# Sign of converted 64-bit weights: carried by ScalarE's slope for negative numbers instead of a VectorE step

## The chip, the cores and the metric

The kernel runs on one core of a Trainium2 chip. The metric is the device time of one execution in microseconds (us). Each time is told with its source: the median of several runs, or one profiled execution with its trace.

## The reference

All inputs are drawn on the host; what is computed is

```python
scores = scale * np.matmul(q, k.transpose(0, 1, 3, 2))      # q, k, v: (4, 8, 576, 64) float32
scores = np.where(block_i >= block_j, scores, -1e9)         # blocks of 64 positions
attn = softmax(scores)                                      # max subtracted, sum + 1e-9
x = matmul(attn, v) -> (2304, 512)
x = (1 / (1 + np.exp(-(x @ w_gate))) * (x @ w_val)) @ w_out # w_gate, w_val: (512, 1536), w_out: (1536, 512)
p = probs / (probs.sum(-1) + 1e-9)                          # (2304, 4)
for e in range(4):
    out += p[:, e:e+1] * (np.maximum(x @ w1[e], 0) @ w2[e]) # w1: (4, 512, 1024), w2: (4, 1024, 512)
```

The three weights of the gated stage (w_gate, w_val, w_out) are multiplied by a 64-bit scalar when they are drawn, so they arrive as 64-bit floats. The kernel gets their raw words and has to make 32-bit floats of them on the chip. The other inputs are 32-bit.

## The kernel before, in words

There are three stages. Attention works on 16 pairs of heads, four for each of the four batches; scores, row maximum, exponential, normalisation, transposition and the product with v follow each other in a software pipeline (`attn_items`). The gated stage runs in four passes, one for each batch of 576 tokens, over 12 blocks of 128 of the 1536 columns (`l1_1`, `l2_1`). The last stage runs over the four experts in three passes of 768 tokens. The first layers of both dense stages use seven products where a plain two-by-two block product has eight, and each product is made of three matmuls of high and low parts, so that weights and activations are split into two parts (`split_sb`, `split3`).

Attention, the conversion of weights and the first gated pass run together, ahead of about 340 us. Five of the 12 column blocks are converted beside the first batch's attention (`NC0 = 5`), the other seven during pass 0, one stretch of steps after each product; `w_out`'s block for f is loaded and converted in pass 0 as well (`wo_get`). The converted and split weights go to DRAM and are read back in the later passes, so passes 1 to 3 and the last stage convert nothing.

One column block takes two conversions (w_gate and w_val), each of a raw tile of 128 partitions by 512 numbers of two 32-bit words, and w_out one more: 12 x 3 = 36 calls of `from_f64`. A call has four steps, which work on the words in place:

- line 477, ScalarE: the high word, read as a 32-bit float, is multiplied by 2^-112. This corrects the exponent's bias by eight times 112. The sign bit stays at the top.
- line 478, VectorE: the low word is shifted right by 29 bits.
- line 479, VectorE: the high word is shifted left by 3 bits and or-ed to it. The shift drops the sign and the two highest bits of the exponent field.
- line 481, VectorE: the sign bit of the high word, which still stands there, is masked out and or-ed in.

GpSimd then forms differences of the quarter blocks (line 527). `split_sb` makes high parts on ScalarE (line 110) or GpSimd (line 108) and low parts on VectorE or GpSimd (line 112), and SyncE's queue stores them (lines 535, 556). The raw tiles rotate through three buffers, and their loads (lines 512, 554) go out on SyncE.

VectorE also holds, ahead of 340 us, the row maxima (line 308), the sums of the softmax (lines 334, 335), the differences for attention's low parts (lines 209 to 233), the additions that evacuate products (lines 676, 732) and the gate's products (lines 686, 689). ScalarE holds the exponentials (line 310), the copies out of PSUM (lines 347, 672) and the gate's Relu, Tanh, Exp and Abs (lines 682 to 685).

The code gives an order by costs (`_merge`, `attn_to`). The order on each engine, however, is made when the program is built, by a planner that simulates the times of the instructions (`TC_ARGS` in line 34 asks for this); a semaphore holds an instruction until what it reads is there, and each engine works through its own list in order.

Of the kernel before, what the change touches and what calls it, by code (L numbers as in the profile page):

```python
# [8 lines left out]
F32 = mybir.dt.float32  # L9
F32R = mybir.dt.float32r  # L10
I32 = mybir.dt.int32
AF = mybir.ActivationFunctionType
ALU = mybir.AluOpType
# [44 lines left out]
def attention_moe_moe_kernel(  # L58
# [13 lines left out]
    nc = tc.nc  # L72
# [398 lines left out]
    def from_f64(bits, out=None):  # L471

        lo, hi = bits[:, :, 0], bits[:, :, 1]
        f = lo if out is None else out.bitcast(I32)
        nc.scalar.activation(out=hi.bitcast(F32), in_=hi.bitcast(F32), func=AF.Copy, scale=2.0 ** -112)
        nc.vector.tensor_scalar(out=f, in0=lo, scalar1=29, scalar2=None, op0=ALU.logical_shift_right)
        nc.vector.scalar_tensor_tensor(
            out=f, in0=hi, scalar=3, in1=f, op0=ALU.logical_shift_left, op1=ALU.bitwise_or)  # L480
        nc.vector.scalar_tensor_tensor(
            out=f, in0=hi, scalar=-(1 << 31), in1=f, op0=ALU.bitwise_and, op1=ALU.bitwise_or)
        return f.bitcast(F32)

    wg = {}
# [20 lines left out]
    def conv_items(f):  # L506
# [9 lines left out]
        def f64(gv):  # L516
            d[gv] = from_f64(d["raw", gv].rearrange("p c f t -> p (c f) t"))
# [30 lines left out]
    def wo_get(p, f):  # L548
        t = wo[f] = moe1.tile([P, 2, DM], F32R, tag="wo", name="wo", bufs=4)
        if p:  # L550
            nc.sync.dma_start(out=t.bitcast(F32), in_=wo_d[f])
            return
        raw = conv.tile([P, NKT, P, 2], I32, tag="raw", name="raw", bufs=3).rearrange("p c f t -> p (c f) t")
        nc.sync.dma_start(out=raw.rearrange("p d t -> p (d t)"), in_=w_out.bitcast(I32)[f * P:(f + 1) * P, :])
        split_sb(t[:, 0], t[:, 1], from_f64(raw), "a", "p")
        nc.sync.dma_start(out=wo_d[f], in_=t.bitcast(F32))
# [547 lines left out]
```

## Time and profile before

| | |
|---|---|
| median of 3 runs | 1487.22 us (1484.6 to 1490.24) |
| profiled execution, its own time | 1486.85 us |
| its span, first to last instruction | 1485.1 us |
| TensorE matmuls | 1416.2 us busy (95%) |
| TensorE weight loads | 1258.9 us busy (85%) |
| VectorE | 977.0 us (66%), 2123 instructions |
| ScalarE | 840.1 us (57%), 2089 instructions |
| GpSimd | 546.8 us (37%), 570 instructions |
| mean granted TensorE clock | 0.985 of full speed |

The table's shares are means over the whole span, in which the stages differ. How to read the views: a stage's busy times are read against the length of the stage. The chain of waits goes back from the last instruction of a window, at each step to what released it or to the instruction before it on its engine. "A <- B" in a list of waits means that A's engine stood idle until B was done. In rows, PE is TensorE, PEld its weight loads, DVE VectorE, ACT ScalarE, POOL GpSimd, SPq SyncE's DMA issues; L481 is line 481.

### The profile page before, as it was taken

To read this page: it belongs to the slowest core of one execution; us is meant where nothing else is said; L and a number is where in the kernel's file an instruction comes from. 1 tells how busy PE (TensorE), PEld (TensorE's weight loads), DVE (VectorE), ACT (ScalarE), POOL (GpSimd) and SP (SyncE) were. 2 spreads that over 40 slices of the span, in tenths; PEclk is the share of its full clock that TensorE was granted. 3 is DMA by queue.
4 is the path that set the end of the run, shared out by engine and by line. 5 is a ranking of instruction groups with operands and counts; after the bars stand their busy time and mean duration, and the time that the engine had idled before them with its cause. 6 is when DMAs were issued, how large, how long until landed. Compare 5 with 4: busy or idle time off the path is not lost.

```text
span 1485.1 us, 24042 instructions
## 1 busy us (share of the span) xinstructions
PE 1416.2 (95%) x8288; PEld 1258.9 (85%) x8288; DVE 977.0 (66%) x2123; ACT 840.1 (57%) x2089; POOL 546.8 (37%) x570
## 2 busy tenths in 40 slices
PE   7877998889999999999999999999999999999998
PEld 3455887777899999989998998989989988989897
DVE  5877899888746755885665565665555666545553
ACT  5787888878965665764544444454444444444431
POOL 5964557443210100230343333544334344344330
PEclk9988999989999999999999999999999999999999
DMA  7896898777668988896322112242121222122201
GB/s 212 244 295 199 273 306 287 254 258 240 206 211 270 303 275 279 272 367 240 118 76 81 58 63 66 82 146 71 57 71 67 76 87 100 61 68 76 80 30 43
DMA packets 176489, 243.84 MB, mean 164 GB/s; under 512 B 71152, under 2 KB 123376, under 8 KB 176368
## 3 DMA queue, kind: packets, MB, share of 16 engines
q1 hardware_dynamic: 176368, 242.30, 50.0%
q8 instruction: 66, 1.08, 0.3%
q14 instruction: 55, 0.45, 0.1%
HBM read 199.79 MB, written 42.47 MB: 163 GB/s over the span
## 4 chain that ended last, share of the span: by engine, by line
PE 78%; DVE 8%; ACT 5%; DMA 3%; POOL 2%; issue 2%; SPq 1%; DVEq 0%; POOLq 0%; ACTq 0%
PE c L98 34%; PE o L98 26%; PE lo L98 8%; PE s L98 3%; PE obank L98 3%; PE tbank L360 2%; DMA wr<-in_moe_w_dram 1%; ACT pt L310 1%; PE t L98 1%; DVE r L686 1%; POOL wt L824 1%; DVE nm L308 1%; DVE xc L112 1%; PE tbank L195 1%; DMA raw<-in_moe_w_gate_dram 1%
## 5 line engine op out<-in xcount | busy, mean ns | idle before, releaser
L98 PE MATMUL o<-w,hb 128*128 128x512 f32 x1728 | 434.5, 392 | 2.1 <-ACT hb L881 1.0
L98 PEld LDWEIGHTS o<-w,hb 128*128 128x128 f32 x1728 | 322.1, 188 | 58.8 <-ACT hb L881 1.3
L98 PE MATMUL c<-xc,w1g 128*128 128x384 f32 x1728 | 341.6, 338 | 0.7 <-ACT xc L110 0.4
L98 PEld LDWEIGHTS c<-xc,w1g 128*128 128x128 f32 x1728 | 308.8, 188 | 18.1 <-ACT xc L110 1.1
L824 POOL TENSOR_TENSOR wt<-wr 128x256 f32<-128x256 f32 x96 | 90.4, 962 | 460.0 <-DMA wr<-in_moe_w_dram 374.7
L98 PE MATMUL lo<-g,wo 128*128 128x288 f32 x1008 | 171.6, 303 | 15.0 <-DVE x L732 7.7
L882 DVE SCALAR_TENSOR_TENSOR hb<-c,hb 128x384 fp32r<-128x384 f32 x192 | 133.6, 708 | 61.2 <-ACT hb L881 61.1
L98 PEld LDWEIGHTS lo<-g,wo 128*128 128x128 f32 x1008 | 144.0, 190 | 22.4 <-DVE x L732 10.0
L872 ACT ACTIVATE snap<-c 128x384 f32<-128x384 f32 x144 | 68.0, 490 | 142.3 <-PE c L98 139.1
L338 POOL TENSOR_SCALAR pt<-pt,nm 128x128 f32<-128x128 f32 (+2 forms) x144 | 91.4, 643 | 146.1 <-DVE nm L335 66.9
L881 ACT ACTIVATE hb<-c 128x384 fp32r<-128x384 f32 x192 | 96.1, 514 | 71.2 <-PE c L98 43.5
L915 DVE SCALAR_TENSOR_TENSOR acc<-o,pr_t,acc 128x512 f32<-128x512 f32 x126 | 92.1, 748 | 66.0 <-PE o L98 64.3
L763 POOL TENSOR_TENSOR w<-wr,w 128x1024 fp32r<-128x1024 f32 x48 | 117.0, 2455 | 31.0 <-ACT w L760 31.0
L760 ACT ACTIVATE w1g<-wt 128x512 fp32r<-128x512 f32 x96 | 60.3, 629 | 78.5 <-PE c L98 62.4
L763 DVE TENSOR_TENSOR w1g<-wt,w1g 128x512 fp32r<-128x512 f32 x96 | 73.3, 765 | 46.9 <-ACT w1g L760 46.6
L879 DVE TENSOR_TENSOR c<-c,snap 128x384 f32<-128x384 f32 x144 | 75.7, 552 | 40.6 <-ACT snap L872 37.3
L763 DVE TENSOR_TENSOR w1g<-wr,w1g 128x512 fp32r<-128x512 f32 x48 | 36.8, 766 | 87.5 <-ACT w1g L760 87.0
L676 DVE TENSOR_TENSOR c<-c,snap 128x288 f32<-128x288 f32 x120 | 54.5, 454 | 52.2 <-PE c L98 35.0
L98 PE MATMUL c<-xc,wa 128*128 128x288 f32 x540 | 84.3, 300 | 4.6 <-DVE c L676 1.4
L98 PE MATMUL c<-xc,wc 128*128 128x288 f32 x504 | 83.4, 301 | 3.0 <-ACT snap L672 3.0
L672 ACT ACTIVATE snap<-c 128x288 f32<-128x288 f32 x126 | 51.4, 408 | 56.5 <-PE c L98 56.0
L760 ACT ACTIVATE w1g<-wr 128x512 fp32r<-128x512 f32 x48 | 30.3, 631 | 92.2 <-DMA wr<-in_moe_w_dram 86.8
(138 smaller groups left out, 2558.1 us busy)
## 6 DMA issues: line engine op xcount, KB each, us to landing
wr<-in_moe_w_dram SPq DMA_DIRECT2D x96, 512.0 KB, 3.5
wa<-wcd SPq DMA_DIRECT2D x48, 512.0 KB, 4.5
wb<-wcd SPq DMA_DIRECT2D x48, 512.0 KB, 5.2
wc<-wcd SPq DMA_DIRECT2D x48, 512.0 KB, 4.4
wo<-wod SPq DMA_DIRECT2D x36, 512.0 KB, 5.7
wd<-wcd SPq DMA_DIRECT2D x48, 256.0 KB, 4.2
raw<-in_moe_w_gate_dram SPq DMA_DIRECT2D x12, 512.0 KB, 4.8
raw<-in_moe_w_val_dram SPq DMA_DIRECT2D x12, 512.0 KB, 4.4
```

The source lines that it names most:

```text
L98: ins = nc.tensor.matmul(out=out, lhsT=lhsT, rhs=rhs, start=start, stop=stop, skip_group_check=skip)
L338: nc.gpsimd.tensor_scalar(out=p, in0=p, scalar1=nm[:, 2 + x:3 + x], scalar2=1.0, op0=ALU.mult, op1=ALU.mult)
L672: nc.scalar.activation(out=t, in_=d["c1"][:, :TH1], func=AF.Copy)
L676: nc.vector.tensor_tensor(out=c, in0=d["c2"][:, :TH1], in1=d[n], op=ALU.add)
L760: nc.scalar.activation(out=hi, in_=src, func=AF.Copy)
L763: (nc.vector if eng_lo == "v" else nc.gpsimd).tensor_tensor(out=lo, in0=src, in1=hi.bitcast(F32), op=ALU.subtract)
L824: nc.gpsimd.tensor_tensor(out=v(t[:, n]), in0=x, in1=y, op=ALU.subtract)
L872: nc.scalar.activation(out=t, in_=d["c1"][:, :TH], func=AF.Copy)
L879: nc.vector.tensor_tensor(out=c, in0=d[tag][:, :TH], in1=d[n], op=ALU.add)
L881: nc.scalar.activation(out=t[:, 0], in_=c, func=AF.Relu)
L882: nc.vector.scalar_tensor_tensor(out=t[:, 1], in0=c, scalar=0.0, in1=t[:, 0].bitcast(F32), op0=ALU.max, op1=ALU.subtract)
L915: nc.vector.scalar_tensor_tensor(out=acc[tt, t], in0=ps, scalar=prs["t"][:, ti, e:e + 1], in1=acc[tt, t], op0=ALU.mult, op1=ALU.add)
```

## The change

The scaling on ScalarE becomes a Prelu with the same scale: numbers of zero and above are multiplied by 2^-112, negative ones by 2^-112 and by a slope of 2^32 besides. A negative number's exponent field is thereby 32 higher, and this bit, shifted left by 3 in line 479, is the sign bit of the result. The last VectorE step is taken out. Count, shape and place of the other steps in the code stay, and so do loads, buffers and stores.

```diff
         lo, hi = bits[:, :, 0], bits[:, :, 1]
         f = lo if out is None else out.bitcast(I32)
-        nc.scalar.activation(out=hi.bitcast(F32), in_=hi.bitcast(F32), func=AF.Copy, scale=2.0 ** -112)
+        nc.scalar.activation(out=hi.bitcast(F32), in_=hi.bitcast(F32), func=AF.Prelu, scale=2.0 ** -112, alpha=2.0 ** 32)
         nc.vector.tensor_scalar(out=f, in0=lo, scalar1=29, scalar2=None, op0=ALU.logical_shift_right)
         nc.vector.scalar_tensor_tensor(
             out=f, in0=hi, scalar=3, in1=f, op0=ALU.logical_shift_left, op1=ALU.bitwise_or)
-        nc.vector.scalar_tensor_tensor(
-            out=f, in0=hi, scalar=-(1 << 31), in1=f, op0=ALU.bitwise_and, op1=ALU.bitwise_or)
         return f.bitcast(F32)
```

## Rows read from the trace of the kernel before

**Rows 1.** Busy us by engine (instructions) in five stages, granted clock, DMA share, GB/s.

```profile
0.00:95.00 95.00, 74.38 (x353) 41.71 (x353) 70.11 (x203) 67.10 (x201) 75.98 (x107) 0.93 0.79 236
95.00:170.00 75.00, 62.14 (x375) 48.52 (x375) 56.45 (x164) 60.63 (x182) 35.45 (x48) 0.89 0.76 236
170.00:340.00 170.00, 152.31 (x1065) 131.59 (x1063) 156.10 (x414) 141.73 (x413) 93.83 (x109) 0.96 0.86 286
340.00:420.00 80.00, 76.05 (x549) 66.15 (x545) 58.31 (x190) 70.11 (x218) 21.47 (x34) 1.00 0.64 196
420.00:1485.00 1065.00, 1051.34 (x5956) 970.91 (x5954) 636.05 (x1155) 500.52 (x1081) 320.04 (x274) 1.00 0.39 131
```

**Rows 2.** TensorE's waits, 170 to 340 us: us in total, times, longest.

```profile
PE lo L98 <- DVE nm L334: 3.5, 2, 2.9
PE lo L98 <- DVE x L732: 3.4, 4, 1.3
PE c L98 <- DVE c L676: 2.7, 3, 1.4
PE lo L98 <- DVE g L112: 2.5, 2, 1.9
```

**Rows 3.** Groups by line, VectorE, to 345 us: busy us, mean ns, idle before.

```profile
L481 DVE SCALAR_TENSOR_TENSOR raw<-raw 128x512 int32<-128x512 int32 x36 | 29.1, 808 | 0.1
```

**Rows 4.** Line 481 alone: ns min/median/max, first and last start, who waited.

```profile
L481 DVE SCALAR_TENSOR_TENSOR raw<-raw x36: 664/686/1554, 18.4 to 333.2; 128x512 int32<-128x512 int32 x36
...
  POOL wt L527: 11.3, 4
```

**Rows 5.** Line 481's busy us (instructions) in a stage, granted clock, DMA.

```profile
170.00:340.00 170.00, 15.71 (x20) 0.96 0.86 286
```

**Rows 6.** Chain of waits followed back from 345 us, line 481: start, us.

```profile
20.93 0.60 DVE raw L481
...
38.12 0.98 DVE raw L481
...
64.98 1.02 DVE raw L481
...
67.78 1.27 DVE raw L481
...
134.62 0.93 DVE raw L481
...
218.57 0.69 DVE raw L481
...
277.17 0.70 DVE raw L481
...
306.96 1.16 DVE raw L481
```

**Rows 7.** The same chain in the narrower window of 200 to 240 us.

```profile
222.47 0.58 DVE raw L481
```

**Rows 8.** Busy us by engine around the longest stall, columns as in Rows 1.

```profile
310.00:323.00 13.00, 7.56 (x37) 6.97 (x38) 9.98 (x25) 7.51 (x22) 7.08 (x8) 0.61 0.75 269
```

**Rows 9.** Groups by line and shape, ScalarE, to 345 us: columns as in Rows 3.

```profile
L477 ACT ACTIVATE raw<-raw 128x512 f32<-128x512 f32 x36 | 24.5, 685 | 3.3 <-DMA raw<-in_moe_w_gate_dram 2.2 <-DMA raw<-in_moe_w_val_dram 1.0
L310 ACT ACTIVATE pt<-s,nm 128x512 f32<-128x512 f32 x26 | 18.0, 690 | 1.2 <-DVE nm L308 1.1
L347 ACT ACTIVATE pTb<-tbank 128x512 f32<-128x512 f32 x24 | 14.4, 598 | 1.0 <-PE tbank L360 0.7
L685 ACT ACTIVATE t<-t 128x288 f32<-128x288 f32 x23 | 10.1, 440 | 0.0
L110 ACT ACTIVATE g<-c 128x288 fp32r<-128x288 f32 x22 | 8.7, 449 | 3.8 <-DVE c L689 3.7
L203 ACT ACT_TABLE_LOAD x1 | 1.3, 1283 | 0.7 <-PEq L1088 0.7
```

**Rows 10.** VectorE in order of time from 18 us: start, us.

```profile
18.07 0.42 DVE L478 TENSOR_SCALAR raw<-raw 128x512 int32<-128x512 int32 x1
```

## The prediction

> **What bounds the kernel now.** I read the busy shares in stages of the span first. From 420 us on TensorE is busy 1051 of 1065 us, and none of the touched lines runs there; from 340 to 420 us it is busy 95%. Before 340 us it is not: 74.4 of 95 us, 62.1 of 75, and 152.3 of 170 [rows 1]. So TensorE stands idle for 51 us ahead of 340 us, and only there can the change act. In 170 to 340 us VectorE is busy 156.1 of 170 us, more than TensorE itself; ScalarE has 141.7, GpSimd 93.8. In 95 to 170 us VectorE (56.5) is behind ScalarE (60.6), and in 0 to 95 us GpSimd (76.0) leads [rows 1]. Next I asked who ends TensorE's waits in 170 to 340 us: four VectorE lines (334, 732, 676, 112) with 3.5 + 3.4 + 2.7 + 2.5 = 12.1 us [rows 2]. None of them is a conversion step: TensorE waits for softmax, evacuation and gate steps that stand in VectorE's queue behind conversions. The reader is to see a queue, not a dependence.
>
> **The step that goes.** Line 481 runs 36 times, 29.1 us, mean 808 ns [rows 3]. Its median is 686 ns, its longest 1554 ns [rows 4]; 36 x 0.686 = 24.7 us is the work, and the 4.4 us above it is stretch, which another step in the same place may pay instead. VectorE thus loses 24.7 to 29.1 of its 282.7 us ahead of 340 us [rows 1]. Twenty of the 36 and 15.7 us lie in 170 to 340 us [rows 5]. On this stretch the Trainium skill has a rule that bears on the size: by "SBUF — State Buffer", section on SBUF's two separate sides, VectorE with two SBUF operands and GpSimd lock each other out of a shared port for a whole instruction. A maximum at more than twice the median agrees with that. By that rule the lock moves to the next two-operand step and the lower end counts; by the row's mean it is the upper one.
>
> What of it is on the path? Busy time alone does not say so. I took the chain of waits followed back from 345 us: line 481 stands on it in eight pieces of 0.60 us or more, 0.60 + 0.98 + 1.02 + 1.27 + 0.93 + 0.69 + 0.70 + 1.16 = 7.35 us [rows 6]. A ninth of 0.58 us shows in a narrower window [rows 7]. Together 7.93 us, or 27% of the line's 29.1 us; the other 73% lies beside TensorE, ScalarE or transfers. The chain is a first-order price. It is too high where a second chain is close behind: with line 481 gone the block is ready at line 479, GpSimd's differences (line 527), which waited 11.3 us for 481 [rows 4], start then, and ScalarE, busy 83% in the crowded stage [rows 1], is late next with its copies and exponentials. It is too low where a queue pile-up also costs TensorE its clock. In 310 to 323 us TensorE was busy 7.56 of 13 us with a granted clock of 0.61 [rows 8], so for a large part at 1.2 instead of 2.4 GHz, behind a stretch in which VectorE was full. There 5.4 us are idle, and the clock costs up to 7.56 x 0.39 = 2.9 us: 8.4 us for one pile-up. I let the two corrections cancel and take 7.9 us.
>
> **The ScalarE step that changes.** Line 477 keeps its count, place and shape: 36 times 685 ns [rows 9]. Prelu is not in the trace before. Nearest rows for another function on the same kind of operands: Abs at 128x288 takes 440 ns against 449 ns for Copy [rows 9], 9 ns less, so -0.3 us in 36. If the new form carries a per-partition operand as the exponential does, the price is 690 - 598 = 92 ns at 128x512 [rows 9], or 3.3 us on ScalarE, all of it late at worst. I take 0, by the row of the plain function; the ends are -0.3 and +3.3 us.
>
> A second price can come with a new function: a table load. The trace has exactly one, of 1283 ns, for Copy, Exp, Relu, Tanh and Abs together [rows 9]. If Prelu is served by what is loaded, nothing is added. The Trainium skill, "ScalarE: Activation LUTs", section "Table sets: the hidden batching unit", speaks against taking this for granted: functions load in named sets, and a change of set costs about 2.66 us with its drain. It names relu, copy, identity and abs as in every set, not Prelu. By that rule two switches for each of 36 blocks would be an estimated 192 us of ScalarE. The one load agrees that five functions share a set; no row shows where Prelu is.
>
> **Moves.** No DMA, buffer or wait is added. The wait of the last step is taken over by line 479, with the same things queued behind it. The three raw tiles come free some 0.7 us earlier for each block, so SyncE's loads may go out earlier, in the same order. But the order on the engines is not that of the code: the second block's line 478 starts at 18.07 us [rows 10], ahead of the first block's line 481 at 18.4 [rows 4]. A planner orders each engine's work by simulated times, and a step less changes its input, so other steps can swap places. The trace has a price for that only in pile-ups like the one above, gained or lost.
>
> **Sum.** 1486.85 - 7.93 + 0 = 1478.9, taken as 1479 us. The profiled execution (span 1485.1 plus 1.75 us around it) lies 0.4 us under the median of 1487.22 us, so the forecast is 0.55% under the median. About 0.5%, or 7.4 us, is what a measurement here can tell from no change: the edge is near 1479.8 us, inside the forecast's own range of 1475 to 1483 us.
>
> **The rivals.**
> - Cover: neighbour chains take over outside the crowded stage, since in 95 to 170 us ScalarE is the fuller engine and in 0 to 95 us GpSimd. Then only the chain pieces after 170 us count: 0.69 + 0.58 + 0.70 + 1.16 = 3.1 us, which gives 1484 us. For it: no TensorE wait names a conversion. Against it: VectorE steps stand back to back on the chain.
> - The crowded stage opens: the 15.7 us freed after 170 us exceed TensorE's 12.1 us of waits for VectorE, and all of these go; with the pieces before 170 us (0.60 + 0.98 + 1.02 + 1.27 + 0.93 = 4.8 us) that is 16.9 us: 1470 us. For it: VectorE at 92%, and the half clock that goes with the waits. Against it: ScalarE is close behind.
> - Other side, pile-ups by the new order: the planner puts more conversion steps ahead of a gate or evacuation step, and TensorE stalls as at 310 to 323 us, at 8.4 us each. One new one cancels the gain; from the second on the kernel is slower: 1478.9 + 2 x 8.4 = 1496 us.
> - Other side too, table loads: two for each of 36 blocks, 72 x 1.283 = 92.4 us. ScalarE's 269.5 us ahead of 340 us would become 361.9, so at least 22 us more: 1509 us. It decides from about 55 loads on, which use up ScalarE's 70.5 idle us.
> - That VectorE's step does not go is excluded: the sign needs no operation but the scaling itself.
>
> **How the numbers follow.** Forecast 0.46, of which 0.26 lies under the edge; cover 0.21; opened stage 0.19; pile-ups 0.10, half of it beyond +0.5%; loads 0.04. Faster: 0.26 + 0.19 = 0.45. Same: 0.20 + 0.21 + 0.05 = 0.46. Slower: 0.05 + 0.04 = 0.09. The range goes from 1468, just below the opened stage, to 1492 us, which holds the cover case with ScalarE's 3.3 us and part of the pile-ups.
>
> **What would show it.** Right: two VectorE steps for each block; VectorE's busy time ahead of 340 us lower by 25 to 29 us; line 477 near 685 ns; one table load; TensorE's waits for VectorE in the crowded stage well under 12 us; the stage from 420 us on as long as before, and the whole shift already there when it begins. Wrong: line 477 at 780 ns or more; more than one load; a second stretch with a granted clock near 0.6 and VectorE full; or VectorE relieved as said while TensorE's idle time ahead of 340 us stays at 51 us.

## The result, and the profile after

The changed kernel takes 1470.5 us (median of 4 runs, 1467.9 to 1472.4) against 1486.1 us for the kernel before (median of 4, 1484.6 to 1490.24). The medians lie 15.6 us apart; the ratio on record is 0.9883, with a 95% interval of 0.9867 to 0.9900, which stands for 15 to 20 us. The forecast was 1479 us, with 1475 to 1483 us as its own range. The direction was right and the time lies in the whole range of 1468 to 1492 us, but the gain is about twice the forecast one: the price of the freed step was mis-sized.

Of the changed kernel's profiled execution (span 1469.3 us), first the busy times by stage, with the columns of [rows 1] (the last stretch ends with the span, after 1049 us):

```profile
0.00:95.00 95.00, 78.38 (x374) 43.96 (x374) 63.36 (x197) 67.33 (x203) 74.96 (x109) 0.86 0.84 255
95.00:170.00 75.00, 62.51 (x376) 50.51 (x375) 58.45 (x166) 64.28 (x193) 38.56 (x52) 0.86 0.80 249
170.00:340.00 170.00, 161.17 (x1160) 140.08 (x1159) 146.62 (x431) 154.36 (x454) 94.86 (x114) 1.00 0.90 298
340.00:420.00 80.00, 77.31 (x557) 67.21 (x557) 52.76 (x164) 63.61 (x192) 16.50 (x25) 1.00 0.61 187
420.00:1485.00 1065.00, 1034.56 (x5829) 956.11 (x5827) 626.41 (x1132) 489.36 (x1049) 317.80 (x272) 1.00 0.38 127
```

The stretch up to 340 us as a whole, first before and then after:

```profile
0.00:340.00 340.00, 288.83 (x1790) 221.83 (x1790) 282.67 (x780) 269.47 (x793) 205.25 (x262) 0.93 0.82 261
0.00:340.00 340.00, 302.07 (x1906) 234.55 (x1907) 268.43 (x794) 285.97 (x849) 208.38 (x273) 0.93 0.86 275
```

By 340 us TensorE has been busy 302 us where it had been 289, with 1,906 matmuls behind it instead of 1,790. Both stages ahead of 170 us are part of this, not the crowded one alone. The granted clock is better in the crowded stage (1.00 for 0.96), worse in the first two (0.86 and 0.86 for 0.93 and 0.89), and 0.93 for the whole stretch in both kernels, so a higher granted clock is not where the time came from.

The conversion's two remaining VectorE steps, and ScalarE's two groups, with the columns of [rows 3]; all to 345 us:

```profile
L479 DVE SCALAR_TENSOR_TENSOR raw<-raw 128x512 int32<-128x512 int32 x36 | 28.6, 800 | 1.2 <-ACT raw L477 0.8
L478 DVE TENSOR_SCALAR raw<-raw 128x512 int32<-128x512 int32 x36 | 21.1, 586 | 7.2 <-DMA raw<-in_moe_w_gate_dram 5.5 <-DMA raw<-in_moe_w_val_dram 1.5
```

```profile
L477 ACT ACTIVATE raw<-raw 128x512 f32<-128x512 f32 x36 | 24.3, 683 | 4.7 <-DMA raw<-in_moe_w_gate_dram 3.4 <-DMA raw<-in_moe_w_val_dram 1.1
...
L203 ACT ACT_TABLE_LOAD x1 | 1.3, 1283 | 0.7 <-PEq L1086 0.7
```

The group of [rows 3] is gone, the others cost about what they did (lines 479 and 478 had 28.7 and 20.5 us before). Prelu takes 683 ns where Copy took 685 [rows 9], and there is still one table load. TensorE's waits in 170 to 340 us, to be read beside [rows 2]:

```profile
PE tbank L195 <- ACT pTb L347: 1.9, 2, 1.4
PE tbank L195 <- ACT pTa L347: 1.2, 1, 1.2
PE s L98 <- ACT pt L310: 1.0, 2, 0.6
PE lo L98 <- ACT wo L110: 0.9, 1, 0.9
PE c L98 <- ACT snap L670: 0.9, 2, 0.7
...
PE lo L98 <- DVE nm L334: 0.3, 1, 0.3
PE lo L98 <- DVE x L730: 0.3, 1, 0.3
...
PE c L98 <- DVE nm L334: 0.2, 1, 0.2
```

The 12.1 us of waits for four VectorE lines have become 0.8 us (line 730 is the former 732); ScalarE heads the list. On its face this is the rival "the crowded stage opens", which had 1470 us. The experiments say otherwise.

### The profile page after: what moved, and what is told of

The parts are those of the page before. It is cut to its first block, busy times and chain, and to the rows that moved or that the text cites. A ratio compares the mean times of both kernels' runs of the same rounds, so it can differ in the third digit from the quotient of the medians.

```text
span 1469.3 us, 24007 instructions
## 1 busy us (share of the span) xinstructions
PE 1413.9 (96%) x8288; PEld 1257.9 (86%) x8288; DVE 947.6 (64%) x2087; ACT 838.9 (57%) x2089; POOL 542.7 (37%) x570
## 4 chain that ended last, share of the span: by engine, by line
PE 80%; DVE 7%; ACT 4%; DMA 4%; POOL 2%; issue 2%; SPq 1%; POOLq 0%; DVEq 0%; ACTq 0%
PE c L98 36%; PE o L98 27%; PE lo L98 8%; PE s L98 3%; PE obank L98 3%; PE tbank L360 2%; PE t L98 1%; DMA xr<-x2d 1%; DMA wr<-in_moe_w_dram 1%; DVE xc L112 1%; DMA raw<-in_moe_w_gate_dram 1%; ACT pt L310 1%; DMA raw<-in_moe_w_val_dram 1%; DVE nm L308 1%; DVE raw L478 1%
## 5 line engine op out<-in xcount | busy, mean ns | idle before, releaser
L338 POOL TENSOR_SCALAR pt<-pt,nm 128x128 f32<-128x128 f32 (+3 forms) x144 | 95.9, 673 | 134.5 <-DVE nm L335 70.7
```

The lines of the kernel that those rows point to most:

```text
L338: nc.gpsimd.tensor_scalar(out=p, in0=p, scalar1=nm[:, 2 + x:3 + x], scalar2=1.0, op0=ALU.mult, op1=ALU.mult)
```

## The experiments

The planner gave every engine a new order for the changed kernel, so the pair differs in two ways: a step less, and another order. To part them, most of the runs below have each engine's list written out, as a chain of ordering edges without a wait. "The old order" is the one that the planner made for the kernel before. Each time is the median of 4 to 12 executions, followed by its ratio to the kernel before on the same chip with the ratio's 95% interval. "Us less" and "us more" are this ratio applied to about 1487 us; they are good to about 2 us.

**1. The step gone, in the old order.**

```diff
+def _keep_order(tc, nc):            # ranks of the old plan, for each engine
+    ...
+        for a, b in zip(v[p:p + n], v[p + 1:p + n]):
+            tc.add_manual_dep(ins[b], ins[a].name, nosync, reason="order written out")
...
         attention_moe_moe_kernel(tc, *args)      # as changed
+        _keep_order(tc, nc)
```

> The changed kernel (Prelu, no third VectorE step), with every engine's list written out in the order that the planner made for the kernel before, less the 36 steps. Queue theory (VectorE's time is what pays, in any order): 1470 to 1474 us, 12 to 16 us under before, and TensorE's waits for VectorE in 170 to 340 us nearly gone. Order theory (about half of the gain comes from the planner's new order): 1477 to 1480 us, the 8 us of the prediction. If the order is all: 1484 to 1487 us.

Measured: 1472.5 us, ratio 0.9894 (0.9881 to 0.9908), 15.7 us less, as the queue theory had it. The sign that went with it, waits for VectorE nearly gone, did not come (experiment 4). The order is not where the gain came from; its own part, some 2 us against the changed kernel, is not resolved by the two intervals.

**2. The new order, the step put back.** The kernel before, with the changed kernel's lists and each line 481 behind its line 479.

> The kernel before (Copy, with the sign step), with every engine's list in the order that the planner made for the changed kernel, and each sign step right behind its line 479. Queue theory: no gain is left, 1484 to 1488 us. Order theory: 1477 to 1480 us, half of the gain without a freed step. A plan made without the step may also suit it badly: then over 1488 us.

Measured: 1490.2 us, 1.0017 (1.0005 to 1.0030). Without the freed step the new order gives nothing; it even costs some 2.5 us, the third case of the expectation. The two runs together settle queue against order. No run writes out the old order for the kernel before itself. That the writing out costs nothing is shown only indirectly: such a cost would stand twice in the sum of experiment 4's two parts and once in the whole, and the two agree within the intervals.

**3. The function alone.**

```diff
-        nc.scalar.activation(..., func=AF.Copy, scale=2.0 ** -112)
+        nc.scalar.activation(..., func=AF.Prelu, scale=2.0 ** -112, alpha=2.0 ** 32)
...
         nc.vector.scalar_tensor_tensor(      # the sign step, kept
             out=f, in0=hi, scalar=-(1 << 31), in1=f, op0=ALU.bitwise_and, op1=ALU.bitwise_or)
```

> Prelu in the place of Copy, and the sign step kept, in the planner's order, which is the same as before. Both theories: the function costs nothing, 1485 to 1487 us, line 477 at 683 to 687 ns. If ScalarE's function matters, 92 ns a time, up to 3.3 us more.

Measured: 1487.4 us, 0.9991 (0.9981 to 1.0000), line 477 at 683 ns. The function is free.

**4. Where the gain arises: the step gone in a part of the blocks, old order.**

```diff
+        calls[0] += 1
+        if calls[0] > 10:            # the other run: <= 10
             nc.vector.scalar_tensor_tensor(...)      # the sign step
```

> Prelu everywhere, the sign step left out only in the first 10 blocks, those beside the first batch's attention; every engine's list as before, less these 10 steps. If the early blocks are worth what the chain of waits gave for them (3.9 us) or are caught up later: 1483 to 1487 us. If the 7 us that the kernel in the old order is ahead by 95 us are theirs and stay to the end: 1480 to 1482 us.

> The counterpart: the sign step left out only in the other 26 blocks, lists as before. By the chain of waits (4.1 us): 1484 us. If the lead that the old order gains after 95 us (8.4 us) is theirs and the two parts add: 1478 to 1481 us. If the crowded stage alone makes the gain, as the prediction's rival had it (12.1 us): 1475 to 1477 us, and then nothing is left for the first 10.

Measured: 1481.0 us, 0.9953 (0.9938 to 0.9968), for the first 10 blocks, and 1478.3 us, 0.9942 (0.9930 to 0.9955), for the other 26: 7.0 and 8.6 us less, 15.6 together. The parts add up to the whole within the intervals, and the 10 early blocks, ahead of the crowded stage, bring almost half. Since the lists of experiment 1 are those of the kernel before, each instruction can be paired with itself by its rank. The lead of ScalarE's instructions over their partners:

| at (us, kernel before) | 95 | 170 | 340 | 480 | 1400 |
|---|---|---|---|---|---|
| lead with the step gone | 7.2 | 9.6 | 15.6 | 15.0 | 15.2 |

The lead grows by 7.2, 2.4 and 6.0 us in the three stages and is not given back after 340 us. The same stages in busy times, of the run with the old order, cut at the instructions that stand at 95, 170 and 340 us in [rows 1]:

```profile
0.00:88.00 88.00, 69.03 (x355) 40.33 (x357) 60.10 (x193) 67.22 (x201) 73.48 (x107) 0.86 0.84 252
88.00:160.40 72.40, 61.16 (x375) 46.91 (x376) 52.94 (x159) 60.34 (x181) 34.36 (x47) 0.91 0.79 245
160.40:324.50 164.10, 151.60 (x1065) 131.97 (x1063) 141.21 (x394) 140.57 (x412) 89.51 (x110) 0.97 0.90 297
```

TensorE's waits in 170 to 340 us of the same run:

```profile
PE lo L98 <- DVE nm L334: 3.5, 1, 3.5
PE s L98 <- ACT tk L222: 2.7, 2, 1.9
PE lo L98 <- DVE g L112: 2.7, 2, 1.8
...
PE lo L98 <- DVE x L730: 1.0, 2, 0.7
```

TensorE's busy time takes part in the lead as well as its idle time. Up to the 340 us point it is busy 281.8 us for the 288.8 us before, with as many matmuls (1,790), and idle 42.7 us for 51.2; of the 7.0 us won in the first stage 5.4 are busy time, at a granted clock of 0.86 for 0.93. Since the profile models where pipelined matmuls end, this split is rough, and its cause is not shown.

In the list of waits the VectorE lines keep 7.2 of the 12.1 us, and yet the time is within 2 us of the changed kernel, which has 0.8 left. (Counted from 160 us on, where the stage begins in these faster runs, it is 7.9 against 3.1 us.) So the sum of TensorE's waits for VectorE is no price either: in this pair another order changed which engine ends a wait, and hardly the time.

**5. The step doubled.** First in the planner's own order, then in the old one.

```diff
         nc.vector.scalar_tensor_tensor(
             out=f, in0=hi, scalar=-(1 << 31), in1=f, op0=ALU.bitwise_and, op1=ALU.bitwise_or)
+        nc.vector.scalar_tensor_tensor(
+            out=f, in0=hi, scalar=-(1 << 31), in1=f, op0=ALU.bitwise_and, op1=ALU.bitwise_or)
```

> The kernel before with the sign step a second time behind the first (the second changes nothing in the data), in the planner's own order: 25 to 29 us more on VectorE. Queue theory: VectorE at 92% in the crowded stage has no room, so at least as much is lost as the change gained, 1502 to 1512 us. Chain price (27% of the line's time): 1494 us. Order theory: anywhere within 8 us of 1494 us.

> The sign step twice, as in the run before with a second step, but in the old order with the second right behind the first. If the loss of 10 us there was small because the planner made room: 1501 to 1506 us, the 15 us of the change with the other sign. If the price is smaller upward whatever the order: 1496 to 1500 us.

Measured: 1498.2 us, 1.0067 (1.0055 to 1.0080), in the planner's order, and 1514.3 us, 1.0177 (1.0162 to 1.0192), in the old one: 10 and 26.3 us more. Of the first expectation the queue theory missed, and the chain price by 4 us; only the order theory's wide band (1486 to 1502 us) holds the time. The second missed in both cases. The first loss is smaller than the queue theory had it, because the planner made room: 16 us lie between the two orders. The second is larger than the gain with its sign turned: a second step costs nearly its whole time (29.5 us), the first was worth half.

**6. Time, operands or wait: another step in its place, old order.** The step becomes a maximum over single elements, which leaves the data as it is and reads one operand; then the same on the high words, which nobody reads any more, so that the readers wait for line 479; then over half of the elements.

```diff
-        nc.vector.scalar_tensor_tensor(
-            out=f, in0=hi, scalar=-(1 << 31), in1=f, op0=ALU.bitwise_and, op1=ALU.bitwise_or)
+        nc.vector.tensor_reduce(     # second run: hi for f; third: f[:, :256]
+            out=f.bitcast(F32), in_=f.bitcast(F32).rearrange("p (n t) -> p n t", t=1), axis=AX.X, op=ALU.max)
```

> Prelu everywhere; in the place of the sign step stands one that changes nothing in the data, a maximum over one element each of 128x512, in place: the same wait, the same place in every list, about the same time on VectorE (some 690 ns), but one SBUF operand instead of two. If VectorE's time and place are all that pays: 1486 to 1490 us and GpSimd's instructions as long as before. If part of the gain is that GpSimd is no longer held off by a two-operand step: 1479 to 1484 us, with GpSimd's instructions ahead of 340 us some 8 us shorter in sum, as they are where the step is gone.

> As the run with a one-operand step, the same lists and the same time on VectorE (some 676 ns each), but the step works in place on the high words, which nobody reads any more: the block's readers wait for line 479 only. If VectorE's time is what pays (a queue): 1482 to 1486 us, as with the step in the path. If the wait of the block's readers pays (a dependence): near the run with the step gone, 1472 to 1476 us.

> As the run with a one-operand step, over 256 of the 512 elements, so some 400 ns instead of 676. If each microsecond of VectorE's time has the same price (12 us for 24): 1478 to 1480 us. If the price rises with the load (26 us were lost by a second step, 15.5 gained by the first): 1474 to 1477 us.

Measured: 1483.9 us, 0.9977 (0.9965 to 0.9989), in the path; 1479.8 us, 0.9952 (0.9937 to 0.9968), beside it; 1478.8 us, 0.9941 (0.9926 to 0.9957), half as long: 3.4, 7.1 and 8.8 us less than before. The first run's step, and its busy times up to the instruction that stands at 340 us before:

```profile
L481 DVE TENSOR_REDUCE raw<-raw 128x512 f32<-128x512 f32 x36 | 24.3, 676 | 0.1
```

```profile
0.00:335.00 335.00, 287.46 (x1790) 222.32 (x1790) 278.21 (x780) 268.63 (x793) 197.07 (x262) 0.93 0.84 264
```

The one-operand step takes 676 ns on the mean where the two-operand one took 808 [rows 3], and GpSimd's 262 instructions take 197.1 us where they took 205.3 [rows 1]; with the step gone they take 197.4. (With a second two-operand step they stay at 205.4, so this is no simple sum.) So the sign step and GpSimd's instructions did hold each other up, by 4.8 us on VectorE and 8 on GpSimd, as the Trainium skill has it in "SBUF — State Buffer", section on SBUF's two separate sides; here it was worth 3.4 of the 15.7 us. The trace of the kernel before shows it instruction by instruction. The longest sign step began while GpSimd was in line 112 and ended 0.55 us after that was done:

```profile
253.04 1.29 POOL L112 TENSOR_TENSOR wb<-wt,wb 128x512 fp32r<-128x512 f32 x1
253.32 1.55 DVE L481 SCALAR_TENSOR_TENSOR raw<-raw 128x512 int32<-128x512 int32 x1
```

So it is with all nine sign steps that took 931 to 1554 ns: each ended 540 to 566 ns after the GpSimd instruction that was running when it began. The other 27 took 664 to 695 ns. Of the 36 maxima 14 began beside a running GpSimd instruction, and none took more than 690 ns. The number of operands alone does not decide it, though: line 478 reads one operand (429 ns median), and its longest (1521 ns) began beside a GpSimd instruction too and ended 287 ns after it.

The second run came out between its two expectations, the third (1478.8 us) where every microsecond of VectorE has the same price. Busy times of the second and of the third run, cut in the same way:

```profile
0.00:330.00 330.00, 285.52 (x1791) 219.10 (x1792) 274.15 (x781) 268.51 (x794) 199.35 (x263) 0.94 0.84 269
```

```profile
0.00:332.00 332.00, 288.00 (x1790) 220.77 (x1790) 268.69 (x780) 268.39 (x793) 197.53 (x262) 0.94 0.84 267
```

The second run's VectorE is busy 274.2 us, 4 us less than the first run's, though its step takes the same 676 ns, so what the wait of the readers costs by itself stays open; by the ratios 3.7 us lie between the two runs.

**7. A check on what the runs add up to.** Set out by VectorE's busy time up to the same 340 us point, the kernels in the old order lie near one curve, on which a point was still to be had (the two of experiment 4, with 274.0 and 264.5 us and 7.0 and 8.6 us less, lie within about 2 us of it):

```diff
         nc.vector.scalar_tensor_tensor(...)      # the sign step, whole
+        nc.vector.scalar_tensor_tensor(
+            out=f[:, :256], in0=hi[:, :256], scalar=-(1 << 31), in1=f[:, :256], op0=ALU.bitwise_and, op1=ALU.bitwise_or)
```

> The kernel before with the sign step a second time over 256 of the 512 elements, right behind the first, in the old order: some 14 us more on VectorE ahead of 340 us, about 297 us. If the price of VectorE's time rises with its load (0.5 us each at 254 to 269 us busy, 0.76 at 278 to 283, 1.0 beyond 283): 12 to 15 us more than before, 1499 to 1502 us. If there is one price, the mean of the gain (15.7 us for 28.4): 8 us more, 1495 us, and the second whole step's 26 us is a jump of its own.

Measured: 1502.4 us, 1.0104 (1.0090 to 1.0118): 15.5 us more, just beyond the upper end of the rising price and nearly twice what one price gives. Its busy times and those of the whole second step, cut in the same way:

```profile
0.00:356.50 356.50, 297.30 (x1791) 225.94 (x1792) 301.28 (x815) 270.14 (x793) 203.03 (x262) 0.92 0.78 249
```

```profile
0.00:363.00 363.00, 298.87 (x1790) 227.60 (x1790) 308.90 (x814) 269.49 (x790) 205.38 (x262) 0.89 0.77 244
```

| old order | VectorE busy, us | against before, us | price of each us to the next row |
|---|---|---|---|
| step gone | 254.3 | -15.7 | 0.5 |
| half a step, one operand | 268.7 | -8.8 | 0.3 |
| step beside the path, one operand | 274.2 | -7.1 | 0.9 |
| step in the path, one operand | 278.2 | -3.4 | 0.8 |
| before | 282.7 | 0 | 0.8 |
| step and a half | 301.3 | +15.5 | 1.4 |
| two steps | 308.9 | +26.3 | |

Each difference is good to about 2 us, so single prices are rough, and within the upper five rows no rise is clear. Clear is that all of the time below today's load has a price of 0.55 (15.7 us for 28.4) and the time above it 0.8 to 1.0 (15.5 for 18.6, 26.3 for 26.2). The two last rows lack one or two records in the trace.

Not all of the higher price is VectorE's queue. In the two last rows TensorE is busy 297.3 and 298.9 us with matmuls that took 288.8 us before, at a granted clock of 0.92 and 0.89 for 0.93. That is 8.5 of the 16.5 us, and 10.0 of the 23.0 us, by which the 340 us point comes later there; the rest is idle time. In the rows above "before" the granted clock is 0.93 or 0.94. And the price holds for a fixed order: in the planner's own, the second step cost 10 us.

**8. Further down the curve.** The changed kernel, with line 479 working on the high word alone and line 478 left out.

```diff
-        nc.vector.tensor_scalar(out=f, in0=lo, scalar1=29, scalar2=None, op0=ALU.logical_shift_right)
-        nc.vector.scalar_tensor_tensor(
-            out=f, in0=hi, scalar=3, in1=f, op0=ALU.logical_shift_left, op1=ALU.bitwise_or)
+        nc.vector.tensor_scalar(out=f, in0=hi, scalar1=3, scalar2=None, op0=ALU.logical_shift_left)
```

> The changed kernel, with the lowest three bits of the 23 of each converted weight left out: lines 478 and 479 become one shift of the high word, one operand, about 430 ns. 49.7 us of VectorE become some 15.5. If VectorE's time goes on paying half of itself: 17 us less than the changed kernel, 1453 to 1457 us. If ScalarE, at 91% in the crowded stage after the change, now sets the pace: 1462 to 1468 us.

Measured: 1460.8 us, 0.9829 (0.9811 to 0.9847), 8 us under the changed kernel by the ratios and 10 by the medians, between the two expectations. The one step that is left (line 478 in this kernel) has the expected 430 ns as its median, but 571 on the mean, since it is held up as before; so 20.5 us are left and not 15.5:

```profile
L478 DVE TENSOR_SCALAR raw<-raw 128x512 int32<-128x512 int32 x36 | 20.5, 571 | 5.7 <-ACT raw L477 5.4
```

Its VectorE, in the planner's own order, up to 316 us:

```profile
0.00:95.00 95.00, 77.42 (x391) 44.42 (x392) 57.28 (x191) 69.76 (x210) 71.46 (x110) 0.89 0.88 272
95.00:160.00 65.00, 57.29 (x350) 45.30 (x350) 47.51 (x145) 58.41 (x176) 35.13 (x46) 0.89 0.81 244
160.00:316.00 156.00, 147.00 (x1036) 129.31 (x1035) 124.02 (x368) 137.24 (x401) 86.22 (x107) 0.97 0.89 298
```

That is 228.8 us, 25 less than with the step gone, at a price of 0.3 to 0.4 for each: the curve seems to go on flattening, though this point has an order of its own. ScalarE is busier than VectorE in all three stages there. It is the fastest kernel of the study, but its converted weights lack the lowest three of 23 bits.

## Why the prediction was right or wrong

- **What bounds the kernel: right.** All of the gain arises ahead of 340 us and stays to the end; VectorE's load is what pays. That only TensorE's 51 us of idle time could shrink does not fit what the profile counts: idle time gave 8.5 us and busy time 7.0.
- **The count: right.** VectorE's busy time ahead of the 340 us point fell by 28.4 us in the old order, within 25 to 29. It is near the upper end, so the stretch of line 481 went with it and did not move to line 479 (788 ns on the mean there, 798 before); line 478 took over a part (629 for 570).
- **ScalarE's function: right.** 683 ns, no second table load, no measurable time. The Trainium skill's rule in "ScalarE: Activation LUTs", section on table sets, which names relu, copy, identity and abs as in every set, did not bite: the one load of 1283 ns serves Prelu too.
- **The order: right that it changes, and its price is small here.** Neither a pile-up nor a gain: some 2 us, not resolved. That holds for this change only; with a step added, two orders lie 16 us apart.
- **The price of the step: wrong, and this is the term that failed.** The prediction took line 481's own pieces on the chain of waits, 7.93 us or 27% of its 29.1 us, and let two corrections cancel; the other 73% it took to lie beside other work and to be worth nothing. In the same order, with nothing else changed, the step was worth 15.7 us, 54%. The chain's price is too low in every stage: 7.2 us for pieces of 3.87 up to 95 us, 2.4 for 0.93 up to 170 us, 6.0 for 3.13 after it. The chain tells on whose instruction the time was spent on one path, with all durations as they were. Taking 36 steps out of a queue also shortened others' (8 us on GpSimd), and let the path leave VectorE: summed over eight windows, VectorE's pieces on the chain fell from 86 us before to 39 us in the run with the old order, though line 481 had only 8 of them. In the changed kernel itself they are 69 us at about the same gain, so how far the path leaves VectorE hangs on the order and does not give the price. The correction upward that the prediction named, TensorE's clock, was not it (0.93 before and after). How much of the missing 8 us each of these makes, beyond the 3.4 us of the mutual holding up, is not settled.
- **"A queue, not a dependence": mostly borne out.** A step of the same kind and length that no reader waits for lies near the same curve; some 4 us may be the readers' wait.
- **The rivals.** The opened stage had the time, 1470 us, and the waits that go, but not the place: it gave 12.1 us to the crowded stage and 4.8 to all before it; the first 10 blocks alone bring 7.0. Its sum came out right by luck, by two terms that were wrong in opposite directions. The cover case failed at its premise, that a stage in which another engine is fuller takes nothing from VectorE's relief: GpSimd led in 0 to 95 us, and most was gained there for each step (7.2 us of lead with 11 of the 36 steps). Pile-ups and table loads did not come.

## What to carry to other kernels

Where several engines are each busy for most of a stage, a line's own pieces on the chain of waits are not a price for all of its time; here, in a fixed order, a microsecond of VectorE's time was worth about half of itself below today's load and nearly all of itself above it, where TensorE's clock fell as well. Price such a step from both sides (the chain below, its busy time above) and choose a value between them, not the lower end. When a planner sets the order, a run with the old order written out tells a freed engine from a lucky plan at the price of one kernel.

## What had not been expected of the hardware

A VectorE bit operation on two SBUF operands and a maximum over one, both 128x512 and in the same place of the same lists, take 808 and 676 ns on the mean, and GpSimd's instructions beside them 205 and 197 us. The difference is in nine of the 36 steps alone, each of which began beside a running GpSimd instruction and ended some 550 ns after it; the longest shift of a single operand behaves in the same way (429 ns median, 1521 longest). ScalarE's Prelu with an immediate slope costs the same as a Copy with a scale, 683 against 685 ns, as the prediction took it without a row for Prelu.
